# Opening loads of an attention and gated-MLP kernel: queries ahead of keys, by halves on two queues

## The chip, the cores and the metric

One core of a Trainium2 chip runs the whole problem. The time is device microseconds of one execution; the figure for a kernel is the median of its runs. The core has five engines that run side by side, each through its own list of instructions in order: TensorE (PE) for matrix products, VectorE (DVE), ScalarE (ACT) and GpSimd (POOL) for elementwise work, and SyncE (SP), which here only issues transfers. ACT and POOL issue transfers too, and an engine that issues one does so in its place in its list. All transfers run on the core's 16 DMA engines.

## The reference, cut to what matters

Grouped attention (16 query heads on 4 key heads), whose result is the input of a gated MLP with a product over the sequence. Batch 8, sequence 384, head width 64, model width 1024; inputs and output are float32.

```python
k = np.repeat(k, group, axis=1)            # group = 16 // 4
v = np.repeat(v, group, axis=1)
scores = scale * np.matmul(q, k.transpose(0, 1, 3, 2))
scores = scores - np.max(scores, axis=-1, keepdims=True)
attn = np.exp(scores)
attn = attn / (np.sum(attn, axis=-1, keepdims=True) + 1e-09)
x = np.matmul(attn, v)                     # then heads side by side: (B, S, 1024)
...
h = np.maximum(x @ w_in, 0.0)
u, v = (h[..., :d_ff // 2].copy(), h[..., d_ff // 2:].copy())
v_n = (v - mu) / np.sqrt(var + 1e-06)      # mean and variance of each row
v_s = np.einsum('ts,bsd->btd', w_spatial, v_n) + b_spatial[None, :, None]
return ((u * v_s) @ w_out).astype(np.float32)
```

## The kernel before

All products are done in float16 with sums in float32. A batch is cut into six sets: three tiles of 128 queries, times two pairs of key heads (j = 0 for heads 0 and 1, j = 1 for heads 2 and 3). Keys and queries have to stand with the head width on the partitions. They are loaded as float32 with the sequence on the partitions, cast to float16 (`cast_k` L187, `cast_q` L208), turned by PE with a product against the identity into PSUM (`k_turn` L226, `q_turn` L240), and copied to `kT` and `qT` (`copy`, L218) by the engine that the call names. From the third batch on the turning is done by transposing transfers.

Then, for each set, a unit of work for each of three key tiles: two score products, one for each key head of the pair (`units`, tile sc, L281); two exponentials on ACT (tile aT, L293); and once the three are there, the weighted sums (`weigh`, tile av, L301) with a column of ones that gives the denominator. DVE divides (L315, L317), PE turns the result (`x_turn`, L334), and the MLP's products (pv L357, pu L438, psp L457, po L495) are poured between the attention's units, in portions of a planned length.

The order in each engine's list is that of the program's text: `tc.manual_schedule()` adds only the waits. A planner inside the kernel keeps an estimate of each engine's clock, by which it chooses which of the eight PSUM banks a tile takes and how much MLP work goes between two units. The first 21 units are issued one or two at a time, the others by threes.

What is in front of the first unit concerns us here. Ten transfers are issued at the start on the queues of SP and ACT (`part` for keys and values, by heads; `part_q` for queries: set of heads j, halves h, query tiles t). PE runs products of zeros meanwhile (`idle(n)`, L609, n of them). The casts of the first keys and queries follow, then the first key turn with its copy on ACT, the first query turn with its copy on DVE, and the scores. The second set's keys (heads 2 and 3) and queries (j = 1) are cast and turned behind the first three units (the `at(2, ...)` calls). On POOL, a load of `w_in` with a cast in it (L163) stands behind the first cast.

Of the kernel before, what the change touches and what calls it, by code (L numbers as in the profile page):

```python
# [18 lines left out]
def kernel(  # L19
# [52 lines left out]
    pool, dve, act, sp = nc.gpsimd, nc.vector, nc.scalar, nc.sync  # L72
# [6 lines left out]
    def bank(shape, dtype, name):  # L79
        i = min(range(8), key=done.__getitem__)  # L80
        t = ps.tile(shape, dtype, name=name, tag=f"bank{i}")
        clock[nc.tensor] = max(clock[nc.tensor], done[i])
        done[i] = 1e12 + clock[nc.tensor]
        taken[name] = i
        return t

    def spend(ns):
        clock[nc.tensor] += ns
# [16 lines left out]
    def stage_tile(n, b, j=None):  # L105
        shape = [P, 2, NT, G * D] if n == "q" else [P, HKV, NT * D]
        t = ld.tile(
            shape, FP32, name=f"{n}32_{b}_{j}", tag=f"{n}32", bufs=5 if n == "q" else 2
        )
        stage[n, b, j] = t  # L110
        return t

    def part(src, t, lo, hi, eng):
        eng.dma_start(t[:, lo:hi, :], src[lo:hi].rearrange("h (p t) d -> p h (t d)", t=NT))
# [7 lines left out]
    def part_q(b, j, hs, ts, eng):  # L122
        h0, h1, t0, t1 = hs[0], hs[-1] + 1, ts[0], ts[-1] + 1
        eng.dma_start(
            stage["q", b, j][:, h0:h1, t0:t1],
            q[b, 8 * j + 4 * h0 : 8 * j + 4 * h1].rearrange(
                "(h i) (c t r) d -> (i c) h t (r d)", i=G, t=NT, r=G
            )[:, :, t0:t1],
        )

    def load_q(b, j, eng=sp, ts=(0, 1, 2)):
# [4 lines left out]
    k0, v0, q00, q01 = (  # L136
        stage_tile("k", 0),
        stage_tile("v", 0),
        stage_tile("q", 0, 0),
        stage_tile("q", 0, 1),  # L140
    )

    part(k[0], k0, 0, 1, sp)
    part(k[0], k0, 1, 2, act)
    part_q(0, 0, (0,), (0,), sp)
    part_q(0, 0, (1,), (0,), act)
    part(k[0], k0, 2, 4, sp)
    part_q(0, 1, (0, 1), (0,), act)
    part(v[0], v0, 0, 2, sp)
    part_q(0, 0, (0, 1), (1,), sp)  # L150
    part_q(0, 1, (0, 1), (1,), act)
# [9 lines left out]
    def load_w_in(half, lo, hi):  # L161
        cols = slice(half * DH, (half + 1) * DH)
        pool.dma_start(  # L163
            w_in16[:, lo:hi, cols],
            moe_w_in[lo * P : hi * P, cols].rearrange("(t p) f -> p t f", p=P),
        )
# [13 lines left out]
    k16s, q16s, kTs, qTs = {}, {}, {}, {}  # L180

    def cast_k(b, eng, js=(0, 1), hs=slice(0, 2)):
        if b not in k16s:
            k16s[b] = ld.tile([P, 2, NT, 2, D], FP16, name=f"k16_{b}", tag="k16")
        src = stage["k", b, None].rearrange("p (j h) (t d) -> p j t h d", h=2, t=NT)
        for j in js:
            eng.tensor_copy(k16s[b][:, j, :, hs], src[:, j, :, hs])  # L187

    def cast_v(b, eng, js=(0, 1)):
        g0, g1 = 2 * js[0], 2 * js[-1] + 2  # L190
# [5 lines left out]
    def cast_q(b, j, eng, ts=None, hs=(0, 1)):  # L196
        if (b, j) not in q16s:
            q16s[b, j] = ld.tile([P, NT, G, 2, D], FP16, name=f"q16_{b}_{j}", tag="q16", bufs=4)
        t16 = q16s[b, j]
        src = stage["q", b, j].rearrange("p h t (r d) -> p h t r d", d=D)  # L200
        for hh in hs:
            if ts is None:
                eng.tensor_copy(t16[:, :, :, hh, :], src[:, hh])  # L203
            elif len(ts) > 1:
                t = slice(ts[0], ts[-1] + 1)
                eng.tensor_copy(t16[:, t, :, hh, :], src[:, hh, t])  # L206
            else:
                eng.tensor_copy(t16[:, ts[0], :, hh, :], src[:, hh, ts[0]])  # L208

    def new_kT(b):  # L210
        kTs[b] = att.tile([P, 2, S], FP16, name=f"kT_{b}", tag="kT")

    def new_qT(b, j):
        qTs[b, j] = att.tile([P, NT, G * P], FP16, name=f"qT_{b}_{j}", tag="qT", bufs=4)

    def copy(eng, o, i, name):
        reads(eng, 600.0 if name.startswith("po") else 430.0, name)
        (act.copy if eng is act else dve.tensor_copy)(o, i)  # L218

    def k_turn(b, j, eng):  # L220
        if j == 0:
            new_kT(b)
        name = f"kps_{b}_{j}"
        ps = bank([P, S], FP16, name)
        for t in range(NT):
            nc.tensor.transpose(  # L226
                ps[:, t * P : (t + 1) * P],
                k16s[b][:, j, t].rearrange("p h d -> p (h d)"),
                ident16,
            )  # L230
        spend(NT * C128)
        copy(eng, kTs[b][:, j], ps, name)

    def q_turn(b, j, t, eng):
        if t == 0:
            new_qT(b, j)
        name = f"qps_{b}_{j}_{t}"
        ps = bank([P, G * P], FP16, name)
        for i in range(G):
            nc.tensor.transpose(  # L240
                ps[:, i * P : (i + 1) * P],
                q16s[b, j][:, t, i].rearrange("p h d -> p (h d)"),
                ident16,
            )
        spend(G * C128)
        copy(eng, qTs[b, j][:, t], ps, name)
# [356 lines left out]
    def idle(count):  # L603
        name = f"idle_{idle_no[0]}"
        ps = bank([P, P], FP32, name)
        done[taken.pop(name)] = clock[nc.tensor] + 400.0
        idle_no[0] += 1
        for _ in range(count):
            nc.tensor.matmul(ps, zero16, zero16, start=True, stop=True)  # L609

    cast_k(0, pool, (0,), slice(1, 2))
    load_w_in(1, 0, 4)
    cast_k(0, dve, (0,), slice(0, 1))
    cast_q(0, 0, dve, (0,), (0,))
    cast_q(0, 0, dve, (0,), (1,))
    cast_k(0, pool, (1,))
    idle(25)
    k_turn(0, 0, act)
    idle(4)
    q_turn(0, 0, 0, dve)  # L620
    idle(5)

    cast_v(0, pool, (0,))
# [415 lines left out]
```

## Time and profile before

| | |
|---|---|
| runs | 240.33 us median of 3 (239.26 to 242.33) |
| the profiled execution | 239.11 us, span 237.1 us |
| PE, DVE, ACT, POOL busy | 97%, 61%, 71%, 43% of the span |
| first transfers issued (SP, ACT) | 0.97, 1.01 us |
| first scores on PE, first exponential on ACT | 6.26, 6.67 us |
| first weighted sums | 9.7 us |
| granted PE clock | 1.00 |

The span is the time from the first to the last instruction of the core. A line of the timeline gives the start, the duration of a run of instructions of one kind, the engine (a q behind its name: it issues a transfer; PEld: PE loads weights), the line of the kernel, the operation, what it writes and reads, how many there are, and in brackets how long the engine stood idle before it and what ended that. In the list of waits a line gives who waited for whom, the sum in us, how often, and the longest.

### The profile page before, as it was taken

What the parts mean: (1) busy time and instruction counts of PE and PEld (TensorE: products, weight loads), DVE (VectorE), ACT (ScalarE), POOL (GpSimd) and SP (SyncE); (2) the same over time, 40 slices, a digit from 0 to 9 for tenths busy, and PEclk for the clock granted to TensorE, in tenths of its full rate; (3) what the DMA queues carried; (4) which work ended last, traced back from release to release, by engine and by line L of the source; (5) the groups of instructions that cost most, each with busy time, mean ns of one, the idle gap of its engine ahead of it and who ended that gap; (6) DMA issues with size and microseconds to landing.
All of it is one profiled execution on the core that took longest, in us unless ns stands there. A gap on an engine that the chain in (4) does not pass through costs nothing.

```text
span 237.1 us, 5939 instructions
## 1 busy us (share of the span) xinstructions
PE 230.1 (97%) x2313; PEld 123.7 (52%) x2313; DVE 144.0 (61%) x382; ACT 169.3 (71%) x349; POOL 102.1 (43%) x149
## 2 busy tenths in 40 slices
PE   7899999999999999999999999999999999999992
PEld 6555655545554546554564555554465455545541
DVE  2668774676456764566656576376645577377462
ACT  2899989968997869977797776985697776402211
POOL 3489583651566343274055700575031500550740
PEclk9999999999999999999999999999999999999999
DMA  6999999999999999989979899479902642340256
GB/s 168 282 319 316 272 145 165 199 292 223 308 227 210 244 374 177 243 240 294 181 230 234 235 211 287 85 250 182 254 3 60 114 174 56 46 177 0 91 212 233
DMA packets 67469, 47.48 MB, mean 200 GB/s; under 512 B 48336, under 2 KB 60416, under 8 KB 67440
## 3 DMA queue, kind: packets, MB, share of 16 engines
q1 hardware_dynamic: 62512, 39.86, 69.9%
q0 software_dynamic: 3952, 6.42, 12.0%
q10 hardware_dynamic: 976, 0.82, 1.2%
q8 instruction: 18, 0.29, 0.5%
q14 instruction: 11, 0.09, 0.1%
HBM read 25.95 MB, written 12.58 MB: 163 GB/s over the span
## 4 chain that ended last, share of the span: by engine, by line
PE 86%; DMA 6%; DVE 2%; SPq 1%; POOL 1%; issue 0%; ACTq 0%; ACT 0%
PE pu L438 17%; PE po L495 17%; PE pv L357 17%; PE sc L281 14%; PE av L301 13%; PE psp L457 6%; DMA q<-in_q_dram 4%; DMA qT<-q 2%; SPq L258 1%; PE qps L240 1%; POOL vn L401 1%; PE xps L334 1%; DVE x L317 1%; DVE qT L218 1%; DVE osb L218 1%; POOL q L206 0%
## 5 line engine op out<-in xcount | busy, mean ns | idle before, releaser
L293 ACT ACTIVATE aT<-sc 128x512 f16<-128x512 f32 x288 | 147.4, 621 | 30.9 <-PE sc L281 30.3
L301 PEld LDWEIGHTS <-aT 128*128 128x128 f16 x1152 | 47.0, 97 | 17.1 <-issue 1.9
L357 PE MATMUL pv<-w_in,xt 128*128 128x512 f16 x192 | 51.0, 380 | 0.1
L301 PE MATMUL av<-v,aT 128*128 128x65 f16 x1152 | 50.5, 193 | 0.0
L495 PE MATMUL po<-w_out,gT 128*128 128x512 f16 (+2 forms) x196 | 50.5, 375 | 0.0
L438 PE MATMUL pu<-xt,w_in 128*128 128x384 f16 x256 | 49.9, 327 | 0.0
L401 POOL TENSOR_SCALAR vn<-vr,rstd,nmr 128x512 f16<-128x512 f32 x23 | 17.6, 779 | 67.0 <-DVE nmr L396 45.6
L474 POOL TENSOR_TENSOR gT<-vs,uT 128x384 f16<-128x384 f32 x31 | 32.4, 1057 | 31.0 <-DVE r_all L315 16.9
L317 DVE TENSOR_TENSOR x<-av,r_all 128x256 f16<-128x256 f32 x96 | 40.8, 424 | 3.3
L281 PE MATMUL sc<-qT,kT 64*128 64x512 f16 x288 | 41.5, 380 | 0.5 <-DVE qT L218 0.2
L315 DVE RECIPROCAL r_all<-av 128x4 f32<-128x4 f32 x96 | 17.1, 179 | 40.5 <-PE av L301 40.1
L218 DVE COPY osb<-po 128x512 f32<-128x512 f32 (+1 forms) x39 | 26.6, 683 | 15.9 <-PE po L495 15.9
L438 PEld LDWEIGHTS <-w_in 128*128 128x128 f16 x256 | 22.1, 98 | 17.1 <-issue 5.5
L449 ACT ACTIVATE uT<-pu 128x384 f16<-128x384 f32 x32 | 15.8, 495 | 16.0 <-PE pu L438 15.8
L495 PEld LDWEIGHTS <-gT 128*128 128x128 f16 x196 | 17.3, 97 | 17.3 <-issue 3.2
L357 PEld LDWEIGHTS <-xt 128*128 128x128 f16 x192 | 15.8, 97 | 17.8 <-issue 5.5
L281 PEld LDWEIGHTS <-kT 64*128 64x128 f16 x288 | 10.9, 94 | 23.7 <-issue 12.3
L457 PE MATMUL psp<-wsT,vn 128*128 128x384 f16 x96 | 22.2, 327 | 0.0
L469 DVE TENSOR_TENSOR vs<-psp,bias_bc 128x384 f32<-128x384 f32 x32 | 17.6, 552 | 7.1 <-PE psp L457 6.9
L203 POOL CAST q<-q 128x768 f16<-128x768 f32 x22 | 17.6, 831 | 9.5 <-DMA q<-in_q_dram 4.5
L371 DVE TENSOR_SCALAR vr<-pv 128x512 f32<-128x512 f32 x24 | 16.4, 683 | 8.4 <-PE pv L357 8.3
L383 DVE BATCH_NORM_STATS2 stats<-vr 128x6 f32<-128x512 f32 x24 | 16.4, 685 | 0.1
(55 smaller groups left out, 101.9 us busy)
## 6 DMA issues: line engine op xcount, KB each, us to landing
out_dram<-osb SPq DMA_DIRECT2D x21, 512.0 KB, 3.2
q<-in_q_dram SPq DMA_DIRECT2D x10, 768.0 KB, 5.9
v_None<-in_v_dram SPq DMA_DIRECT2D x6, 384.0 KB, 5.7
w_in<-in_moe_w_in_dram POOLq DMA_DIRECT2D x4, 512.0 KB, 9.8
k_None<-in_k_dram SPq DMA_DIRECT2D x5, 384.0 KB, 3.7
q<-in_q_dram POOLq DMA_DIRECT2D x2, 768.0 KB, 7.6
out_dram<-osb SPq DMA_DIRECT2D x5, 256.0 KB, 3.1
w_out<-in_moe_w_out_dram POOLq DMA_DIRECT2D x2, 512.0 KB, 8.6
```

Source lines behind the costliest of these rows:

```text
L203: eng.tensor_copy(t16[:, :, :, hh, :], src[:, hh])
L218: (act.copy if eng is act else dve.tensor_copy)(o, i)
L281: nc.tensor.matmul(sc, kTs[b][rows, j, kt * P : (kt + 1) * P], qTs[b, j][rows, qt].rearrange("p (r i c) -> p i r c", r=G, i=G), start=True ...
L293: act.activation(a, sc, AF.Exp, scale=scale)
L301: nc.tensor.matmul(av[:, i * (D + 1) : (i + 1) * (D + 1)], aT[:, kt, hh, i * P : (i + 1) * P], v1[b % 2][:, 2 * j + hh, kt, 0 : D + 1], st ...
L317: dve.tensor_tensor(x16s[b][:, qt, c : c + 256].rearrange("p (i d) -> p i d", i=G), o[:, :, 0:D], r.to_broadcast([P, G, D]), ALU.mult,)
L357: nc.tensor.matmul(pv, xts[b][:, kt, st * P : (st + 1) * P], w_in16[:, kt, DH:DFF], start=(kt == 0), stop=(kt == NK - 1),)
L401: (dve if b == 0 and st == 1 else pool).tensor_scalar(vn, v_r.pop((b, st)), rstd[:, st : st + 1], nmr[:, st : st + 1], op0=ALU.mult, op1=A ...
L438: nc.tensor.matmul(pu[:, 0:S], w_in16[:, kt, m * P : (m + 1) * P], xts[b][:, kt, :], start=(kt == 0), stop=(kt == NK - 1),)
L457: nc.tensor.matmul(psp[:, 0:S], v_n[b, st][:, m * P : (m + 1) * P], wsT16[:, st, :], start=(st == 0), stop=(st == NT - 1),)
L474: pool.tensor_tensor(gT, vs, uT, ALU.mult)
L495: nc.tensor.matmul(po[:, 0:width], gTs[b][:, m, tt * P : (tt + 1) * P], w_out16[:, m, c0 : c0 + width], start=(m == 0), stop=(m == NM - 1),)
```

## The change

The four loads of the first keys and queries become eight, four on each queue, in the same order on both: one half of the first set's queries, one key head of the first pair, one of the second pair, one half of the second set's queries. The values and the later query tiles follow as they did. The casts are dealt out anew: POOL casts the second half of the queries in place of the second key head, DVE the first half of the queries and then the first key head, ACT the second key head with an activation copy. On PE the first query turn goes ahead of the first key turn, with two products of zeros between them, not four.

```diff
-    part(k[0], k0, 0, 1, sp)
-    part(k[0], k0, 1, 2, act)
-    part_q(0, 0, (0,), (0,), sp)
-    part_q(0, 0, (1,), (0,), act)
-    part(k[0], k0, 2, 4, sp)
-    part_q(0, 1, (0, 1), (0,), act)
+    for h, eng in ((0, sp), (1, act)):
+        part_q(0, 0, (h,), (0,), eng)
+        part(k[0], k0, h, h + 1, eng)
+        part(k[0], k0, 2 + h, 3 + h, eng)
+        part_q(0, 1, (h,), (0,), eng)
     part(v[0], v0, 0, 2, sp)
     part_q(0, 0, (0, 1), (1,), sp)
     part_q(0, 1, (0, 1), (1,), act)
...
-            eng.tensor_copy(k16s[b][:, j, :, hs], src[:, j, :, hs])
+            (act.copy if eng is act else eng.tensor_copy)(k16s[b][:, j, :, hs], src[:, j, :, hs])
...
-    cast_k(0, pool, (0,), slice(1, 2))
+    cast_q(0, 0, pool, (0,), (1,))
     load_w_in(1, 0, 4)
+    cast_q(0, 0, dve, (0,), (0,))
     cast_k(0, dve, (0,), slice(0, 1))
-    cast_q(0, 0, dve, (0,), (0,))
-    cast_q(0, 0, dve, (0,), (1,))
+    cast_k(0, act, (0,), slice(1, 2))
     cast_k(0, pool, (1,))
     idle(25)
+    q_turn(0, 0, 0, dve)
+    idle(2)
     k_turn(0, 0, act)
-    idle(4)
-    q_turn(0, 0, 0, dve)
     idle(5)
```

The sequence of instructions on each engine is otherwise the one of before; the changed kernel's lines behind the loads carry numbers lower by one.

## The prediction

> **What bounds the kernel now.** I read the page's table of engines first, then the idle time of TensorE by what ended it, then the timeline of the first 13 us engine by engine, then the chain that ended last.
>
> ```profile
> span 237.1 us, 5939 instructions
> PE 230.1 (97%) x2313; PEld 123.7 (52%) x2313; DVE 144.0 (61%) x382; ACT 169.3 (71%) x349; POOL 102.1 (43%) x149
> ...
> PE qps L240 <- DVE q L208: 0.3, 1, 0.3
> PE xps L334 <- DVE x L317: 0.3, 1, 0.3
> PE sc L281 <- DVE qT L218: 0.2, 1, 0.2
> PE sc L281 <- DMA qT<-q: 0.2, 1, 0.2
> ```
>
> TensorE (PE) is busy 97% of the span, and behind the first microseconds nothing in its own queue waits over 0.3 us. Its work is a fixed list in a fixed order, so the end can only move by what moves the front of that list. The front is here, ACT and the loads first:
>
> ```profile
> 1.01 0.40 ACTq L114 DMA_DIRECT2D k_None<-in_k_dram  x1
> 1.44 0.93 ACTq L124 DMA_DIRECT2D q<-in_q_dram  x2
> 4.48 0.38 ACTq L124 DMA_DIRECT2D q<-in_q_dram  x1
> 4.90 0.48 ACT L218 COPY kT<-kps 128x384 f16<-128x384 f16 x1 [2.65 <-PE kps L226]
> 6.67 14.89 ACT L293 ACTIVATE aT<-sc 128x512 f16<-128x512 f32 x30 [1.29 <-PE sc L281]
> ```
>
> The third line is the one to look at: ACT's fourth load is issued at 4.48, not behind the third at 2.37, and the copy of kT starts only when that issue is over (4.86), although its transposes (3 in 0.50 us from 3.99) were done at 4.49. An issue that waits holds up ACT's own work. The last line: from 6.67 on ACT does 30 exponentials without a gap, 0.496 us each.
>
> ```profile
> 3.38 0.35 DVE L187 CAST k<-k_None 128x192 f16<-128x192 f32 x1 [2.21 <-DMA k_None<-in_k_dram]
> 4.48 0.68 DVE L208 CAST q<-q 128x256 f16<-128x256 f32 x2 [0.74 <-DMA q<-in_q_dram]
> 5.22 0.53 PE L240 MATMUL qps<-ident,q 128*128 128x128 f16 x4 [0.30 <-DVE q L208]
> 5.78 0.42 DVE L218 COPY qT<-qps 128x512 f16<-128x512 f16 x1 [0.62 <-PE qps L240]
> 6.26 0.82 PE L281 MATMUL sc<-qT,kT 64*128 64x512 f16 x6 [0.24 <-DVE qT L218]
> 7.12 0.50 POOL L187 CAST k<-k_None 128x384 f16<-128x384 f32 x1 [2.24 <-DMA k_None<-in_k_dram]
> 7.30 0.66 DVE L208 CAST q<-q 128x256 f16<-128x256 f32 x2 [1.09 <-DMA q<-in_q_dram]
> 9.65 0.83 PEld L301 LDWEIGHTS <-aT 128*128 128x128 f16 x24
> ```
>
> The first queries land at 4.45 and set the first scores (6.26): cast, turn, copy. Keys for heads 2 and 3 land at 7.08, the second set of queries at 7.28. The first weighted sums (L301) load at 9.65: that is 6.67 plus six exponentials (2.98), to the hundredth. From there PE follows ACT and both run full (PE 12.00 of 12.00 us busy from 12 to 24). So a first score that is x later makes the kernel x longer, and the same the other way.
>
> **The change, part by part.** *Order of the loads.* Each of the two queues now carries 128 KB of queries, then 96 KB of keys, 224 KB in all, as before with keys first. Before, these 224 KB had landed at 4.45 (SP) and 4.64 (ACT). A queue is read in order, so I take 4.45 and 4.6 for the first keys now, and for the queries 0.97 + 2.4 (the 96 KB at the head took that) + 0.27 (32 KB more at 117 GB/s, which is 128 KB from 3.36 to 4.45) = 3.64.
>
> *Casts and the query turn.* DVE casts one half (0.28 to 0.48), POOL the other (0.40, its two later ones): done at 4.1. Four transposes 0.53: 4.6. The key cast on DVE starts at 4.45 (0.35), then the copy of qT (0.42): 5.25. POOL's cast is 0.06 longer than the key cast it replaces and starts about as late, so the weight load behind it (issued 3.88) moves 0.1 to 0.2; the weights are first used at 13.06. All this lies ahead of the key path and costs nothing; if the key path were free, the scores would be 4.6 (keys landed) + 0.31 (ACT's cast: not in this trace; between 0.25 and 0.45; ACT takes 495 ns for 384 and 621 for 512 elements, 1 ns an element, so 0.3 for 192) + 0.05 + 0.34 (three transposes at 7.68) + 0.03 + 0.48 (copy of kT) + 0.06 = 5.9 to 6.05, a gain of 0.2 to 0.35.
>
> *What two more loads do to ACT's queue.* Twelve loads instead of ten now open the program. Eight completion counters are given to them in turn, and a load that reuses one waits at its issue for the earlier user. In the built program, the changed kernel's ACT queue reads:
>
> ```
> L124 DMACopy q_0_0_83<-in_q_dram 128x256
> L114 DMACopy k_0_None<-in_k_dram 128x192 x2
> L124 DMACopy q_0_1_84<-in_q_dram 128x256 [waits DMAHW1_49]
> L124 DMACopy q_0_1_84<-in_q_dram 128x2x256 [waits DMAHW2_49]
> L186 TensorCopy k_0_122<-k_0_None 128x3x64 [waits DMAHW5_49]
> L217 TensorCopy kT_162<-kps_0_163 128x384 [waits PE_49]
> ```
>
> Counter 1 is SP's first key load, counter 2 SP's second (head 2). Before, only the last of ACT's loads waited, for counter 1, the first queries: the issue at 4.48. Now ACT waits for head 2 before it may cast head 1, and that cast stands ahead of the first key turn. Head 2 is 96 KB behind the 224 KB on SP: at 117 GB/s it lands at 4.45 + 0.82 = 5.27, at the rate of the 192 KB that came third before (4.45 to 7.08, 73 GB/s) at 5.77. I take 5.5, the middle, since the weight load that shares the engines starts at the same time as before. Then: issue 0.03 + 0.38 + 0.04, cast 0.31, hand-over 0.05, three transposes 0.34 + 0.03, copy 0.48, 0.06 = 1.72 us, and the scores start at 7.22 instead of 6.26: **0.96 us later**; 0.73 with 5.27, 1.23 with 5.77. SP's own two reissues (query slice 1, last values) wait only for the first queries, 3.64: at most 0.8 later than 2.87 and 3.39, and their data stand behind 448 KB anyway.
>
> *The second set.* Its second half is issued on ACT at 4.45 (before: 1.91). By the row's 3.2 at the least and the 5.8 median of the two later ACT query loads it lands between 7.65 and 10.25; 96 KB and its own 128 KB at 97 GB/s (256 KB from 4.64 to 7.28) behind 4.64 give 7.0, so I take 7.65. One cast 0.30, turn and copy as before (7.97 to 8.94 in the trace): scores at 8.9, and ACT works on the first six until 7.22 + 0.41 + 2.98 = 10.6. Hidden, unless it lands after 9.3. The second slice (issued 4.48 before, landed at 10.66, cast by POOL at 10.70) is issued at 5.5 and lands near 11.7; its cast holds up POOL's second value cast and the loads of k, q and v of the next batch by the same 1.0, as everything that reads them is later by that too.
>
> *Clock.* 25 fillers take 103 ns each at the start (2.58 / 25), eight at 8.20 take 61 (0.49 / 8), while the page grants full clock throughout: the ramp shows only in durations (LDWEIGHTS 151 against 96 ns). In the changed order PE stands still from about 4.8 to 6.25, since two fillers, not four, follow the query turn and the key turn comes late. I price this at nothing. The Trainium skill, "TensorE: Matmul & The Clock Gate", Part 1, says that half speed is the idle state, left after some 3.4 us of work and taken again only after an idle window of that length; by this rule too 1.45 us adds nothing.
>
> *Sum.* -0 for the casts, +0.96 for the key path, nothing given back, since six exponentials still end after the second scores are ready. 239.11 + 0.96 = 240.07 for an execution like the profiled one (span 237.1, 2.0 around it). That one is 1.22 under the median of 240.33, and the runs spread from 239.26 to 242.33; moved to the median, **241.3 us**. No fixed deadline further on takes the shift up: the one DMA wait, 0.2 us at 54.8, hangs on a load that SP issues behind transposes which follow PE.
>
> **Rivals.** *It does what it says.* ACT's two reissues don't hold up the key path, because head 2 lands by 4.5 (break-even: 4.54 + 1.72 = 6.26). For it: both queues deliver 224 KB within 0.2 us of each other, and the ACT queue is emptier than before. Against it: 96 KB in 0.1 us has no row. Not slower: gain 0.2 to 0.35, 240.0.
>
> *Second set late.* Its second half lands at 10.25, the median latency: cast, turn, copy, score and the exponential's 0.41 put ACT's seventh at 12.0 where it stood at 9.65, so 2.3 longer: 242.6. For it: the loads issued at this time took 5.4 to 6.2. Against: those had up to 450 KB ahead of them in their queue, this one 96.
>
> *Clock lost.* The pause of 1.45 us keeps PE slow up to the first sums: the 24 loads of L301 at 103 ns need 2.5 instead of 0.83, with slower scores and turns some 1.8 on top of 0.96: 243.1. Against: pauses of 0.2 to 0.3 did nothing, but none of 1.5 is in the trace.
>
> **How the numbers follow.** Queue held up 0.62; as intended 0.16; second set late 0.13; clock lost 0.09. What a measurement can tell here from no change is about 2%, 4.8 us, and no case reaches it alone; only a late set with a lost clock and the spread of the runs (3 us) does. Faster 0.02, within 2% 0.92, slower 0.06. The range takes the two outer cases and the spread about the median in part: 239.4 to 243.1.
>
> **What would show it.** Right: ACT's fourth issue at about 4.5, its fifth at 5.3 to 5.8, its cast of k behind that, key transposes at 6.1 to 6.5, first scores at 7.0 to 7.5, 30 exponentials without a gap from there, first sums about 1 us later than 9.65. Wrong: scores before 6.26; a gap in the exponentials after the sixth (second set); LDWEIGHTS of 151 ns behind 6 us (clock); or a shift at 10 us that is gone by the end.

## The result, and the profile after

The changed kernel takes 242.24 us (median of 8 runs, 241.13 to 243.12), the kernel before 239.39 us (8 runs, 238.81 to 242.33). The ratio is 1.0102, 95% interval 1.0072 to 1.0132: slower by about 2.4 us, too little for the 2% bound. The forecast was 241.3, slower by 0.96. The profiled execution took 242.23 us, 3.1 more than the profiled one of before.

The head of the page, and, from the list of waits, whom TensorE (PE) waited for:

```profile
span 240.5 us, 5939 instructions
PE 231.4 (96%) x2311; PEld 124.4 (52%) x2311; DVE 143.8 (60%) x381; ACT 170.2 (71%) x350; POOL 102.5 (43%) x149
```

```profile
PE xps L333 <- DVE x L316: 1.4, 2, 1.2
PE kps L225 <- ACT k L186: 1.2, 1, 1.2
```

The span is 3.4 us longer and PE's busy time 1.3. Before, nothing held PE over 0.3 us once it had begun; now two waits of 1.2 stand there. One is the first key turn, which waits for ACT's cast, as forecast. The other, a turn of attention results that waits for DVE, was not forecast.

The timeline of the changed kernel, ACT:

```profile
4.22 0.34 ACTq L124 DMA_DIRECT2D q<-in_q_dram  x1
5.58 0.39 ACTq L124 DMA_DIRECT2D q<-in_q_dram  x1
6.01 0.35 ACT L186 CAST k<-k_None 128x192 f16<-128x192 f32 x1 [3.75 <-DMA k_None<-in_k_dram]
...
8.13 10.13 ACT L292 ACTIVATE aT<-sc 128x512 f16<-128x512 f32 x20 [0.70 <-PE sc L280]
19.20 1.08 ACT L292 ACTIVATE aT<-sc 128x512 f16<-128x512 f32 x2 [0.93 <-PE sc L280]
```

Both held issues are there, at 4.22 and 5.58, and the cast of the key head stands behind the second. The bracket names the keys' landing, which the trace records at 4.38, but the cast starts 0.04 after the issue ends: the queue is what it waited for. From 8.13 there are 20 exponentials without a gap, and then a gap of 0.93 that before did not have.

PE, in the same timeline:

```profile
4.35 0.61 PE L239 MATMUL qps<-ident,q 128*128 128x128 f16 x4 [0.28 <-POOL q L207]
...
6.42 0.50 PE L225 MATMUL kps<-ident,k 128*128 128x128 f16 x3 [1.24 <-ACT k L186]
7.49 1.46 PE L280 MATMUL sc<-qT,kT 64*128 64x512 f16 x6
...
9.82 0.44 PE L239 MATMUL qps<-ident,q 128*128 128x128 f16 x4
10.81 0.61 PE L280 MATMUL sc<-qT,kT 64*128 64x512 f16 x4
11.53 0.83 PEld L300 LDWEIGHTS <-aT 128*128 128x128 f16 x24
...
18.55 0.28 PE L333 MATMUL xps<-ident,x 128*128 128x128 f16 x2 [1.19 <-DVE x L316]
```

The six first scores take 1.46 us; before they took 0.82. Three transposes take 0.50; in before's list, once PE was fast, 0.34. PE runs at half speed up to 9.9: four transposes took 0.61 at 4.35 and take 0.44 at 9.82, and the trace's record of the granted clock begins, with full speed, at 9.93 (before: at 5.53).

And the loads that come late, after and then before:

```profile
7.44 0.75 POOL L162 DMA_DIRECT2D w_in<-in_moe_w_in_dram  x1
8.69 0.29 DVE L207 CAST q<-q 128x256 f16<-128x256 f32 x1 [2.03 <-DMA q<-in_q_dram]
8.93 0.07 DVE L597 MEMSET q<- 128x1 f32 x2
9.04 0.88 SPq L124 DMA_DIRECT2D q<-in_q_dram  x2
...
17.45 0.49 DVE L207 CAST q<-q 128x256 f16<-128x256 f32 x2 [1.65 <-DMA q<-in_q_dram]
```

```profile
8.02 0.88 SPq L124 DMA_DIRECT2D q<-in_q_dram  x2
8.27 0.75 POOL L163 DMA_DIRECT2D w_in<-in_moe_w_in_dram  x1
...
13.85 0.48 DVE L208 CAST q<-q 128x256 f16<-128x256 f32 x2
```

The second set's second half lands at 8.67 and is cast at 8.69 (landings here and below are those that the trace records). Behind that cast DVE fills a column of the buffers for the third query tile (L597), and only then may SP issue that tile's load: at 9.04, where before it was 8.02. Before, it stood ahead of POOL's second weight load (issued 8.27); now that one goes first, at 7.44, since POOL's key cast starts at 5.87 and not 7.12, its keys having come in two loads on two queues. The third tile lands at 17.43 (before: 13.30), DVE stands still 1.65 for it, and PE 1.19 behind DVE.

Where the 3.4 us arise is seen by setting the k-th exponential against the k-th of before: the 1st is 1.5 later, the 19th 1.9, the 25th 3.3, and the last, 200 us on, still 3.3.

### The profile page after: what moved, and what is told of

Same layout as the page of the kernel before. It is cut to its first block, busy times and chain, and to the rows that moved or that the text cites. A ratio compares the mean times of both kernels' runs of the same rounds, so it can differ in the third digit from the quotient of the medians.

```text
span 240.5 us, 5939 instructions
## 1 busy us (share of the span) xinstructions
PE 231.4 (96%) x2311; PEld 124.4 (52%) x2311; DVE 143.8 (60%) x381; ACT 170.2 (71%) x350; POOL 102.5 (43%) x149
## 3 DMA queue, kind: packets, MB, share of 16 engines
q0 software_dynamic: 3952, 6.42, 12.3%
## 4 chain that ended last, share of the span: by engine, by line
PE 81%; DMA 13%; DVE 2%; SPq 1%; issue 0%; POOL 0%; DVEq 0%
PE pu L437 17%; PE pv L356 16%; PE po L494 14%; PE sc L280 13%; PE av L300 13%; PE psp L456 6%; DMA q<-in_q_dram 5%; DMA v_None<-in_v_dram 4%; DMA qT<-q 2%; DMA out_dram<-osb 1%; DMA k_None<-in_k_dram 1%; DVE osb L217 1%; PE qps L239 1%; PE xps L333 1%; POOL vn L400 0%
## 5 line engine op out<-in xcount | busy, mean ns | idle before, releaser
L280 PE MATMUL sc<-qT,kT 64*128 64x512 f16 x288 | 42.2, 385 | 0.2
L448 ACT ACTIVATE uT<-pu 128x384 f16<-128x384 f32 x32 | 15.8, 495 | 16.0 <-PE pu L437 15.8
L356 PEld LDWEIGHTS <-xt 128*128 128x128 f16 x192 | 15.8, 97 | 17.8 <-issue 5.5
```

Of the source, the lines that this page charges most:

```text
L280: nc.tensor.matmul(sc, kTs[b][rows, j, kt * P : (kt + 1) * P], qTs[b, j][rows, qt].rearrange("p (r i c) -> p i r c", r=G, i=G), start=True ...
L356: nc.tensor.matmul(pv, xts[b][:, kt, st * P : (st + 1) * P], w_in16[:, kt, DH:DFF], start=(kt == 0), stop=(kt == NK - 1),)
```

## The experiments

Each shift below is that of the named exponential of the profiled execution against before's. Diffs are against the changed kernel where nothing else is said.

| kernel | first scores, six took | shift of 1st, 25th, last | ratio (95%) |
|---|---|---|---|
| before | 6.26, 0.82 | | |
| after | 7.49, 1.46 | +1.5, +3.3, +3.3 | 1.0102 (1.0072 to 1.0132) |
| e1 ten loads | 6.25, 1.46 | +0.2, +1.2, +1.2 | 1.0026 (0.9998 to 1.0053) |
| e2 slice on SP | 6.07, 0.82 | -0.2, +5.5, +5.5 | 1.0183 (1.0133 to 1.0233) |
| e3 fillers | 7.80, 0.82 | +1.6, +2.4, +3.3 | 1.0097 (1.0063 to 1.0131) |
| e4 rest early | 8.64, 1.46 | +2.6, +3.8, +3.8 | 1.0131 (1.0078 to 1.0185) |
| e5 loads alone | 6.68, 0.82 | +0.4, +2.8, +3.1 | 1.0108 (1.0071 to 1.0145) |
| e6 casts alone | 6.04, 0.82 | -0.2, +0.4, +0.4 | 1.0027 (1.0003 to 1.0051) |
| e7 ten loads, fillers | 6.02, 0.82 | -0.2, +0.3, +0.3 | 1.0022 (1.0001 to 1.0044) |
| e8 slice behind | 6.10, 0.85 | +0.6, +5.3, +5.4 | 1.0244 (1.0188 to 1.0300) |
| e9 weights later | 7.50, 1.10 | +1.3, +2.5, +3.1 | 1.0106 (1.0020 to 1.0193) |
| e10 before, no fillers | 6.34, 1.46 | +0.3, +1.3, +1.2 | 1.0042 (1.0002 to 1.0082) |
| e11 weights first | 6.31, 0.82 | +0.1, +4.0, +4.0 | 1.0189 (1.0096 to 1.0281) |

**Which part carries the loss: loads alone (e5), casts alone (e6).** e5 keeps the eight loads and takes casts, turns and fillers from before; e6 is the other half: before's ten loads with the change's casts and turns.

```diff
 e5 (against before)
-    part(k[0], k0, 0, 1, sp)
...
-    part_q(0, 1, (0, 1), (0,), act)
+    for h, eng in ((0, sp), (1, act)): ...
 e6
-    for h, eng in ((0, sp), (1, act)): ...
+    part(k[0], k0, 0, 1, sp)
+    part(k[0], k0, 1, 2, act)
+    part_q(0, 0, (0,), (0,), sp)
+    part_q(0, 0, (1,), (0,), act)
+    part(k[0], k0, 2, 4, sp)
+    part_q(0, 1, (0, 1), (0,), act)
```

> The change's eight loads in front, with the casts, the turns and the fillers of the kernel before. Queue theory: ACT still issues twice under a wait and its copy of kT comes behind that, at 5.6 to 7.1, so first scores at 6.3 to 7.6; the second set's second half is issued at 4.2 and lands at 8.3 to 9.0; first sums shifted by 0.8 to 2.0 us, ratio 1.005 to 1.011: the loads alone carry the loss. Rival (the casts dealt to three engines and the turned order carry it): first scores at 6.3 or before, ratio under 1.003.

> The kernel before with its ten loads in their old order, and the change's casts, turns and fillers. Queue theory: ACT waits once, until the first queries at 4.45, issues until 4.86, casts 0.35, three transposes 0.5, copy 0.48: first scores at 6.35 to 6.5, 0.1 to 0.2 later; with a fast PE a ratio of 1.000 to 1.002, and up to 1.2 us more if PE is still at half speed at its first scores, as in the kernel with ten loads in the new order. Rival (casts and turns carry the loss): first scores behind 7, ratio 1.008 or more.

The loads alone cost as much as the whole change, 1.0108 against 1.0102. The casts and turns alone begin 0.2 us early and end 0.4 late. The timeline of e5:

```profile
6.15 0.48 ACT L217 COPY kT<-kps 128x384 f16<-128x384 f16 x1 [3.90 <-PE idle L608]
...
13.88 0.40 PE L239 MATMUL qps<-ident,q 128*128 128x128 f16 x4 [0.92 <-POOL q L207]
...
16.70 0.74 DVE L207 CAST q<-q 128x256 f16<-128x256 f32 x2 [0.95 <-DMA q<-in_q_dram]
```

In e5 ACT casts nothing, but its copy of kT waits behind the held issue (over at 6.11), though its transposes began at 4.79. Then come the late landings: the second set's second half at 8.47, its second query tile (the second slice) at 13.02, for which PE stands still 0.92, and the third query tile at 16.67, with 0.79 of PE behind it. In the changed kernel the slice landed at 12.25 and stopped nothing. That the loads alone reach the same end with a front only 0.4 late and PE at full speed says that the held queue at the front, the only loss that I forecast, is no more than a part of what the eight loads do. In e6 the first queries landed at 4.05, in before's profile at 4.46, with the same loads; its scores came only 0.2 earlier, as ACT's cast of keys stands behind the held issue there. For the 0.4 at its end there is one line in its timeline:

```profile
16.88 0.38 PE L357 MATMUL pv<-w_in,xt 128*128 128x512 f16 x1 [0.41 <-DMA w_in<-in_moe_w_in_dram]
```

This is the fifth of the pv products, the first that reads the second weight load. In e6 that load was issued at 8.09 and landed at 16.84; before, it was issued at 8.27 and landed at 16.41, just ahead of its use at 16.45. The first weight load, the one that the changed casts delay (issued 4.69, before 3.88), landed at 12.67 and was waited for by nobody. Why the second one took longer was not tested; POOL issued the next batch's loads 1.2 us earlier in e6 (10.66 for 11.83), beside it.

**The held queue: ten loads (e1), one wait instead of two (e2), the load behind the copy (e8).** e1 puts the queries first with ten loads, so that ACT waits once. e2 gives the last of ACT's loads to SP; e8 puts it behind ACT's copy of kT.

```diff
 e1
-    for h, eng in ((0, sp), (1, act)): ...
+    part_q(0, 0, (0,), (0,), sp)
+    part_q(0, 0, (1,), (0,), act)
+    part(k[0], k0, 0, 1, sp)
+    part(k[0], k0, 1, 2, act)
+    part(k[0], k0, 2, 4, sp)
+    part_q(0, 1, (0, 1), (0,), act)
 e2
-    part_q(0, 1, (0, 1), (1,), act)
     part(v[0], v0, 2, 4, sp)
+    part_q(0, 1, (0, 1), (1,), sp)
 e8
-    part_q(0, 1, (0, 1), (1,), act)
...
     k_turn(0, 0, act)
+    part_q(0, 1, (0, 1), (1,), act)
```

> The changed kernel with ten opening loads as before, only in the new order: first queries by halves, first keys by heads, then the keys of heads 2 and 3 as one load and the second set's queries as one load. Casts and turns as in the changed kernel. Queue theory (what costs the time is that two more loads make ACT wait twice at an issue): ACT waits once, at about 4.2, casts its keys at 4.6, first scores at 6.0 to 6.3, first sums at 9.4 to 9.7, the second query tile's load issued near 8.0; time within 0.3 us of the kernel before, 2.5 us under the changed one. Rival (queries first, or the casts dealt out to three engines, cost the time by themselves): first scores behind 6.8 and a ratio of 1.005 or more.

> The changed kernel with its twelve loads, but the last load on ACT's queue (second query tile of the second set) issued by SP. ACT keeps one waiting issue, at 4.22. Queue theory: ACT casts keys at 4.6 and not 6.0, first scores at 6.0 to 6.3 and not 7.49; the second set's second half is still issued at 4.2 and lands at 8 to 8.7, so the second scores stand at 9.5 to 10 and first sums near 10; a ratio to the kernel before of 1.002 to 1.007. Rival (the second issue's wait is not what holds the cast, the keys' landing is): cast still near 6 and first scores near 7.5, ratio 1.010.

> The changed kernel with the last load on ACT's queue issued behind ACT's copy of kT instead of ahead of its cast; nothing else moved. Queue theory: ACT casts its keys at 4.6, first scores at 6.0 to 6.2, first exponential at 6.5 to 6.9 and not 8.13; the second set's second half still lands at 8.3 to 8.7, so first sums shift by 0.6 to 1.0; if the third query tile again lands behind 16, its stop of PE comes on top. Ratio 1.003 to 1.007. Rival (not the place of the issue but the twelve loads' traffic costs the time): first sums at 11 or later, ratio 1.010.

The timeline of e2, and its longest wait of PE:

```profile
4.51 0.35 ACT L186 CAST k<-k_None 128x192 f16<-128x192 f32 x1 [2.27 <-DMA k_None<-in_k_dram]
6.07 0.82 PE L280 MATMUL sc<-qT,kT 64*128 64x512 f16 x6
...
15.29 0.74 POOL L207 CAST q<-q 128x256 f16<-128x256 f32 x2 [7.13 <-DMA q<-in_q_dram]
```

```profile
PE qps L239 <- POOL q L207: 3.6, 2, 3.3
```

With the second held issue gone from in front of the cast, the cast moves from 6.01 to 4.51 and the scores from 7.49 to 6.07, 0.2 ahead of before. That is the forecast's mechanism, shown; e8 (cast at 4.62, scores at 6.10) and e1 (6.25) say the same. But e2 and e8 end 5.5 and 5.4 us late: the slice of queries that was moved is issued at 6.06 (e2) and 6.81 (e8) instead of 5.58, lands at 15.2 and 15.1 instead of 12.3, and PE stands still 3.3 and 3.1 us. Neither edit moved the slice alone: the wait for head 2 passed to the last load of values, which SP issued at 5.65 (e2) and 6.41 (e8), not 4.08, each 0.02 after head 2 had landed, and which landed at 13.1 and 13.3, not 8.5. In e8 the moved issue waited as well, and held ACT's first exponential back to 7.25.

After these stops the granted clock falls. In e2 (time, busy time of five engines, granted clock, share of the DMA engines, GB/s):

```profile
16.00:17.00 1.00, 0.91 (x6) 0.34 (x6) 0.38 (x1) 0.00 (x0) 1.00 (x3) 0.63 0.53 134
17.00:18.00 1.00, 1.00 (x15) 0.79 (x14) 0.11 (x2) 0.84 (x2) 1.00 (x3) 0.50 0.44 72
...
19.00:20.00 1.00, 1.00 (x16) 0.66 (x14) 0.02 (x1) 0.68 (x2) 1.00 (x3) 0.66 1.09 412
```

Half speed from 16.26 to 19.67 (0.63 in one slice is 0.26 us full and 0.74 half; 0.66 is 0.67 half), 3.4 us in which PE does the work of 1.7. So 3.3 of standing still and 1.7 of half speed make 5.0 of the 5.7 between -0.2 and +5.5.

**The clock at the front: fillers (e3, e7), none (e10).** e3 is the changed kernel with 20 products of zeros, not 2, between the two turns; e7 is e1 with 30, 4 and 7 in place of 25, 2 and 5; e10 is the kernel before without the 34 ahead of the first scores.

```diff
 e3
-    idle(2)
+    idle(20)
 e7 (against e1)
-    idle(25)
+    idle(30)
     q_turn(0, 0, 0, dve)
-    idle(2)
+    idle(4)
     k_turn(0, 0, act)
-    idle(5)
+    idle(7)
 e10 (against before)
-    idle(25)
     k_turn(0, 0, act)
-    idle(4)
     q_turn(0, 0, 0, dve)
-    idle(5)
```

> The changed kernel with 20 products of zeros between the query turn and the key turn in place of 2, so that PE does not stand still from 4.8 to 6.4. Clock theory (PE is at half speed until 9.8 because of the pauses): six scores in 0.8 us and not 1.46, LDWEIGHTS of 96 ns from about 5.5 on, first exponential at 7.9 and not 8.13, second scores 0.5 to 0.9 earlier than 10.81, 0.5 to 0.9 us less than the changed kernel (ratio 1.007). Rival (the clock does not matter, ACT and the second set's landing do): PE fast, yet first sums still at 11.4 or later and a ratio of 1.010.

> The kernel with ten loads, queries first, and the change's casts and turns, with more products of zeros: 30 ahead of the query turn and not 25, 4 behind it and not 2, 7 behind the key turn and not 5, so that PE has no pause over 0.2 us before the first scores. Clock theory: PE is at full speed by the first scores (six in 0.8 us and not 1.46), first scores at 6.1 to 6.3, second scores at 8.7 to 9.0, and the shift of 1.2 us that its sister without these fillers showed is gone: ratio 0.998 to 1.000. Rival (the 1.2 us come from the second set's later landing and not from PE's speed): PE fast, second scores behind 9.5 all the same, ratio 1.002 or more.

> The kernel before without its 34 products of zeros ahead of the first scores; loads, casts and turns as before. Clock theory by itself: PE is at half speed at its first scores (six in 1.46 us and not 0.82, LDWEIGHTS of 151 ns until about 9.5), first scores still at 6.2 to 6.3, since the loads set them, second scores near 9.9 and not 8.94, and all behind later by 0.9 to 1.3 us: ratio 1.004 to 1.005. Rival (PE's speed is hidden behind the exponentials): first sums within 0.3 of 9.65, ratio under 1.002.

First e10, then e7, each from its timeline:

```profile
6.34 1.46 PE L281 MATMUL sc<-qT,kT 64*128 64x512 f16 x6 [0.52 <-DVE qT L218]
10.09 0.73 PE L281 MATMUL sc<-qT,kT 64*128 64x512 f16 x4
```

```profile
8.88 0.61 PE L281 MATMUL sc<-qT,kT 64*128 64x512 f16 x4
...
16.76 0.38 PE L357 MATMUL pv<-w_in,xt 128*128 128x512 f16 x1 [0.16 <-DMA w_in<-in_moe_w_in_dram]
```

e10 starts its scores 0.08 after before's and ends 1.2 us later: a front at half speed costs 1.2 us by itself, in its profile, 1.0042 in its runs. e1 shows the same shape (1.46 at 6.25, then 0.71 at 10.00; its first sums, expected by 9.7, begin at 10.88), and e7, in which PE has no pause but one of 0.18 from its first filler to its first scores, starts early, has its second scores 1.1 us ahead of e1's, and ends 0.3 late, where the 0.16 wait for weights stands. In the runs the two differ by less than their intervals (1.0026 and 1.0022), so the 0.9 us between e1 and e7 is a reading of two profiles only.

In e3 PE is fast as well (0.82), and what half speed cost behind the first scores is gone: its shift is 1.6 at the 1st exponential and at the 19th, where the changed kernel's grows from 1.5 to 1.9. The kernel is no better all the same, 1.0097: head 2 landed at 6.03 in this execution, not 5.56, and ACT's cast came as much later; the third query tile is still late (DVE waits 0.76 for it), and 0.79 more is lost at 53.96 for a value cast, so that the rival was right on the ratio:

```profile
16.32 0.74 DVE L207 CAST q<-q 128x256 f16<-128x256 f32 x2 [0.76 <-DMA q<-in_q_dram]
```

**The third query tile: fills early (e4), weights later (e9), weights first (e11).** e4 puts DVE's fills ahead of the second set's casts; e9 puts POOL's second weight load behind its cast of the second slice; e11 is e7 with the first weight load ahead of POOL's query cast.

```diff
 e4
-    at(2, cast_q, 0, 1, dve, (0,))
     at(2, rest_q, 0)
     at(2, rest_q, 1)
+    at(2, cast_q, 0, 1, dve, (0,))
 e9
-    load_w_in(1, 4, 8)
     cast_q(0, 1, pool, (1,))
+    load_w_in(1, 4, 8)
 e11 (against e7)
-    cast_q(0, 0, pool, (0,), (1,))
     load_w_in(1, 0, 4)
+    cast_q(0, 0, pool, (0,), (1,))
```

> The changed kernel with the two tiny DVE fills that release the loads of the third query tile put ahead of the second set's query casts, so that SP issues these loads at about 5.5 and not at 9.04. Late-load theory (1.2 us of the loss is PE's stop at 18.55, for a query tile that lands at 17.43 because it was issued 1.0 later, into the loads of the next batch): the tile lands before 14, the stop is gone, 1.0 to 1.3 us less than the changed kernel (ratio 1.005). Rival (the transfer engines are full, and an earlier issue only takes time from the second set's queries, which land later than 8.67): first sums later than 11.53 by what the stop gives back, ratio unchanged at 1.010.

> The changed kernel with the second half-megabyte load of w_in on POOL put behind POOL's cast of the second set's second query tile instead of ahead of it (it was issued at 7.44, and at 8.27 in the kernel before). Traffic theory (query tiles issued at or behind that weight load share the transfer engines with it, and that is why the third tile, issued at 9.04, lands at 17.43, while one issued at 8.02 in the kernel before was there by 13.85): the second tile lands by 11 and not 12.3, the third by 15, PE's stop of 1.2 at 18.5 is gone; the weights come 2 to 3 us later and may stop PE once at their first use near 18. Rival (the loads of the next batch, issued on POOL from 13.4 on, are what the third tile meets): it still lands behind 16.5 and the stop remains; ratio 1.010.

> The kernel with ten loads and more fillers, with POOL's first load of w_in put ahead of its query cast (issued near 1.7 and not 4.25). If what was left there (0.3 us behind 16 us) came from the later weights, and the opening loads are not slowed, the front stays 0.2 us early to the end: ratio 0.998 to 1.000. Rival (the weight load takes transfer time from the first queries and keys): first queries behind 4.0, first scores behind 6.4, ratio 1.003 or more.

e4 is inconclusive on the time. The load was issued at 7.22, later than expected, landed at 13.71, not 17.43, and the stop at 18 us is gone; but head 2 landed at 6.71 in this execution, not 5.56, so that its front was 2.6 late, and it ended no better. e9, in its timeline:

```profile
6.59 0.34 PE L225 MATMUL kps<-ident,k 128*128 128x128 f16 x3 [1.69 <-ACT k L186]
7.50 1.10 PE L280 MATMUL sc<-qT,kT 64*128 64x512 f16 x6 [0.29 <-ACT kT L217]
9.03 0.88 SPq L124 DMA_DIRECT2D q<-in_q_dram  x2
...
16.04 0.48 DVE L207 CAST q<-q 128x256 f16<-128x256 f32 x2
```

The third tile is issued at the same time as in the changed kernel (9.03 and 9.04), and with the weights out of its way (issued at 13.40) it lands at 13.31, not 17.43; DVE no longer waits for it. (The second slice, expected by 11, landed at 12.66.) The other executions agree: in all eight with the tile issued ahead of POOL's second weight load (before, e1, e4, e6, e7, e9, e10, e11) it landed by 13.83, in all five with it behind (the changed kernel, e2, e3, e5, e8) at 16.30 or later. That stop is explained. The ratio stays at 1.0106 all the same: PE spent another 3.4 us at half speed at the front, which the last section shows, and later waits again, 0.43 for a value cast at 53.71. e11 was to save e7's 0.16, but that wait was for the second weight load (issued 8.22, landed 16.72), and e11 moved the first. It cost much more: the weights take transfer time from the queries (the first set's second tile, issued at 2.87 in both, landed at 11.87, in e7 at 8.37), and PE waits 2.3 us for DVE's cast of it.

No version beats the kernel before; e7 at 1.0022 is the nearest.

## Why the prediction was right or wrong

**Order, casts, query turn: right.** The queries were there at 3.64 as forecast (cast 3.67) and the first key head by 4.22 (4.45 forecast). The copy of qT ended at 5.42, 0.17 after the forecast, and long before it was needed. The first weights were covered, as forecast: PE waits for none in the changed kernel. That the casts cost nothing at the front holds here, where the held issue comes later; by themselves they took 0.2 us: in e6 the scores follow the first queries by 1.99 us (4.05 to 6.04), before by 1.80.

**ACT's queue: right, and shown.** Issues at 4.22 and 5.58 (4.45 and 5.27 to 5.77 forecast), cast behind them (0.35 for 0.31), scores at 7.49 for 7.22. The step from landing to scores was put at 1.72 and took 1.93 (5.56 to 7.49), mostly because the transposes ran at half speed (0.50 for 0.34). Scores 1.23 later is the upper end that the prediction gave, but it had reached that by a landing at 5.77. That head 2 landed so near the 5.5 of the sum is partly luck: in the seven executions with these eight loads it landed between 5.56 and 6.71. e2 and e8 take the wait away, and the front comes back.

**Clock: the step that failed in kind.** "I price this at nothing" was wrong: half speed made the first exponential 1.46 late where the scores were 1.23 late, and kept PE slow until 9.9. The price of a slow front alone is e10's 1.2 us. The prediction asked whether a pause could send PE back to half speed, and not whether PE had left it: it had worked 2.85 us when the first pause came (1.22 to 4.07), less than the 3.4 us that it had quoted from the Trainium skill ("TensorE: Matmul & The Clock Gate", Part 1). The 2.85 us alone don't decide it: e9 became fast after the same fillers (last section). The rival "clock lost" had the shape right, at 1.8 us and a chance of 0.09, yet it expected slow loads at the first sums. Those run in 0.83 us at 11.53. Of the signs that the prediction named, two of being right failed (20 exponentials without a gap, not 30; first sums 1.9 later, not about 1), and one of being wrong came: weight loads of 151 ns behind 6 us (from 6.50 to 9.82, then 98).

**Second set: hidden from ACT, not from PE.** It landed at 8.67, between the 7.65 that I took and the bound of 10.25, and before the break-even of 9.3. ACT has no gap behind its sixth exponential, so the rival with a late set fell. But from landing to scores it took 2.14, not 1.25, at half speed (1.29 in e2, e3 and e5, where PE was fast), and the first sums, behind these scores in PE's list, begin at 11.53 and not 11.17, where six exponentials end (8.13 and 3.04): 0.4 us that the sum lacked.

**Third query tile: the term that was missing.** The prediction followed the transfers that the diff names, and the second slice, which stayed hidden (landed 12.25, forecast 11.7), though not in e5. The third tile's load is not in the diff. It is released by a fill that stands behind the second set's cast, and it was passed by a weight load that POOL could issue earlier, since its keys landed earlier. Worth 1.4 us here, more than the whole forecast.

**The passing on to the end: right.** What the changed kernel has lost by the 25th exponential is there at the last, to 0.1 us.

So 0.96 became 1.5 (front) + 0.4 (second set) + 1.4 (third tile) = 3.3 in the profiled execution, against 2.4 by the ratio and 2.85 by the medians. The direction and the first mechanism were right; of the size, less than half was in the sum. The stated 241.3 came nearer to the 242.24 than that by luck: it was set on a median of three runs, 240.33, which lies 0.94 above that of eight. The split holds for this execution only. e3 and e9 each cure one term and the ratio doesn't move, as another loss takes the place (a later landing of head 2 in e3, a second slow phase in e9); what every one of them would give with all others cured was not measured.

## What to carry to other kernels

When loads are cut smaller on an engine that also computes, list every issue that reuses a completion counter, and what that engine has queued behind it; then follow also the loads that the diff doesn't name, through whatever releases them. In a kernel whose bound engine works through a fixed list, a loss at the front stays to the end, and moving one late load mostly shows the next. Keep TensorE without a pause until it has become fast, since after a pause it may or may not be (e9 and the changed kernel), and judge that from the durations of equal instructions.

## What the runs showed of the hardware

**Half speed comes back after pauses well under 3.4 us.** e9's PE had been fast: four transposes in 0.46 at 4.33, three in 0.34 at 6.59. Then, in its windows (columns as in e2's; the second number is PE's busy time):

```profile
1.09:4.50 3.41, 3.02 (x27) 2.76 (x28) 0.70 (x4) 1.16 (x1) 1.10 (x6) 1.00 0.71 166
4.50:7.91 3.41, 1.43 (x18) 0.89 (x18) 0.79 (x3) 0.83 (x2) 1.73 (x3) 1.00 1.04 297
...
7.50:8.00 0.50, 0.50 (x6) 0.21 (x6) 0.00 (x0) 0.08 (x1) 0.00 (x0) 0.91 1.42 233
8.00:8.50 0.50, 0.50 (x4) 0.00 (x0) 0.00 (x0) 0.50 (x2) 0.00 (x0) 0.50 0.85 125
...
11.00:11.50 0.50, 0.50 (x4) 0.11 (x2) 0.00 (x0) 0.00 (x0) 0.00 (x0) 0.68 1.11 309
```

Half speed from 7.91 to 11.32, 3.4 us, though PE was at work all that time and its longest pause before was 1.69. In e11 a stop of 2.25 us did the same (half speed from 12.4 to 15.8), in e2 and e8 stops of 3.3 and 3.1. The stop of 1.19 in the changed kernel did not. Within each run the changes of clock that the trace records lie whole steps of 3.41 us apart (e9: 4.50, 7.91, 11.32; e2: 6.02, three steps to 16.26, one to 19.67). In the step before each fall PE was busy 42% (e9), 40% (e11), 15% (e8) and 5% (e2) of the time; in other steps with 64 to 66% it stayed fast (e2, e5, e8, e11, and the changed kernel around its stop of 1.19). The Trainium skill, "TensorE: Matmul & The Clock Gate", Part 1, has half speed return after an idle window of about 3.4 us, in windows that run freely. The length agrees, 3.4 each time; that the window must be idle does not: 1.69 of pause in it was enough.

**The same list can start fast or slow.** Up to the first scores e9 and the changed kernel run the same PE list, with scores at 7.50 and 7.49; e9 was fast from 4.50, the changed kernel not before 9.93. Counted back in steps of 3.41 us, an estimate from the recorded changes, one step of e9 holds nearly all the fillers (1.09 to 4.50, PE busy 88%), while in the changed kernel two steps share them (up to 3.10 and up to 6.51, 55% each). The Trainium skill, "TensorE: Matmul & The Clock Gate", Part 1, calls the moment run-dependent, since the window doesn't start with the kernel; these two executions agree. The busy share does not settle every case: e2 became fast after a step of 91%, at 6.02, e1 not after one of 90%, at 6.60, but one step later. What separates these two stays open.

**The profile's clock row misses the first slow phase.** In the windows of the changed kernel it gives 1.00 from 2.00 to 11.00, while equal instructions took 1.5 to 1.8 times as long as later. The record behind it starts only with the first full speed (9.93). A fall after a fast phase the row does show (e2, e9).

**A load issued a little later can land much later.** The second slice of queries on ACT's queue, by time of issue: 4.48 landed at 10.65 (before), 5.58 at 12.25, 6.81 at 15.08 (e8): 2.3 us later in the queue, 4.4 at the landing, with the DMA engines' busy share at 0.79 or more in each microsecond from 2 to 11 of the changed kernel. The time of issue is not all of it: in e4 the slice was issued at 6.74 and landed at 13.32, and in e8 a load of values had moved as well. e9 shows for the third tile what one transfer ahead of it is worth: 4.1 us at the landing (13.31 for 17.43).
